# Taking the first four steps of a recurrence-and-network kernel apart into single operations, and reordering them

## The chip, the cores and the metric

The kernel runs on one core of one Trainium2 chip. The metric is device time in microseconds. The kernel before takes 613.97 us (median of three runs, 613.32 to 614.89). The engines are named as the profile names them: PE (matrix multiply, with PEld for its weight loads), DVE (vector), ACT (scalar), POOL (GpSimd) and SP (which here only issues transfers). Each works through its own queue of instructions in order, and waits where an instruction needs something that another engine or a transfer has not yet delivered.

## The reference

Two blocks are joined. The first is a gated linear recurrence over 768 time steps for 4 batches of 8 heads of width 48; the second is a network with one hidden layer of 2048 and a leaky activation, applied to its output:

```python
f = 1.0 / (1.0 + np.exp(-f_logit))
for t in range(S):                                  # S = 768
    state = f[:, :, t, :, None] * state + k_t outer v_t
    y[:, :, t] = q_t . state
x = y as (B*S, H*D)                                 # (3072, 384)
h = x @ w_in                                        # (3072, 2048)
g = np.maximum(h, 0.0) + alpha * np.minimum(h, 0.0)
out = g @ w_out                                     # (3072, 384)
```

The weights come in as 64-bit floats and are turned into 32-bit ones on the chip.

## The kernel before

The work is cut into twelve steps. A step is one pair of batches and one chunk of 128 time steps; steps 0 and 1 are the two pairs at the first chunk, steps 2 and 3 the same pairs at the second, and so on. A step has three parts. *Preparation* loads f, q, k and v, takes the sigmoid, builds products of the gates inside groups of four time steps ("lags"), scans over the groups, and forms the scaled q and k. *Attention* makes the scores on PE, copies them under masks, and multiplies with v. *Network* multiplies by `w_in`, applies the activation ("gates") and multiplies by `w_out`.

Each part is a table of small functions with short names. A single string of such names with step numbers gives the order: `FIRST` is written out for all pieces up to step 4's preparation and step 2's network, and `USUAL` is a pattern that repeats from step 4 on. The functions are called in that order, so the place of a name in the string is the place of its instructions in the queue of every engine that it uses. Nothing is reordered later. Semaphore waits are put in where data or a buffer is needed.

The names that matter here, with the lines of the kernel before. A letter `a` or `b` after a name is the half of step 0 (one batch each); a number after the colon is the step; a `V`, `A` or `G` at the end is the engine DVE, ACT or POOL.

- `ld` (L313 to L317) loads f, q, k and two halves of v, five transfers. Step 0 loads on SP's queue, steps 1 to 4 on POOL's. Each of these tiles has one buffer, so the load of f waits for the last reader of the previous step's f.
- `sg` (L320) sigmoid on ACT; `kr` (L321), `qc` (L322), `c0` to `c3` (L345) and `cg` (L347) copies on ACT; `l1`, `l2`, `l3` (recorded under L211, the helper for all elementwise products) the lags, two products each; `sc` (L353, L355) two scans on DVE; `le`, `k4`, `gk`, `nr`, `ke`, `sa`, `sb`, `e2` to `e7` further products at L211.
- `r` (L493), `h` (L553), `x` (L514), `kp` (L571), `of` (L597, L607), `pd`/`pz` (L635), `y` (L694), `t` (L717): the matrix products of attention on PE. `R` (L501) and `X` (L522, L538) are the masked copies of the scores on DVE, `H` (L559, L562) of some of them on ACT, `p` (L680), `oc` (L616, L618) and `s` (L429) the copies into the matrix `A` that `y` reads. `m` (L657 to L670) carries the state on. `z`, `T` and `mv` bring the result into the layout `xT` that the network reads.
- `id0` to `id7` and `jd0` to `jd7` (L235) load one eighth of `w_in` and of `w_out` each, 767 KB, into five buffers on SP's queue; `ih`, `il` (ACT, L240 and L243) and `ib`, `jb` (DVE, L211) turn it into 32-bit floats. A load waits until an earlier piece's `ih`/`il` has freed its buffer.
- The network of step 0 is `na`, `nb` (PE, L781), `ga`, `gb` (ACT, L787), `Ga`, `Gb` (DVE, L793, four instructions each), `va`, `vb` (L823), `o0`, `o1` (the result copies on ACT and their stores on SP). Later steps use `n0` to `n7` (L763), `g0` to `g7` (L769), `G0` to `G7` (L773, two instructions each), the sums `S0`, `S1` (four instructions each), and the products `A1`, `B`, `A2`, `C1`, `C2`, `D`, `E` (L859). `W` are differences of `w_out`, used from step 1 on.
- `kt` turns the keys of steps 2 and later on DVE; `km` moves them with sixteen small transfers on SP's queue, and `pd` waits for these.

So what decides the time of the opening is how five in-order queues, filled from one string, fit each other.

## Time and profile before

| | |
|---|---|
| median of the runs | 613.97 us (613.32 to 614.89) |
| span of the profiled execution, first to last instruction | 613.4 us |
| PE busy | 586.4 us, 96% of the span |
| DVE busy | 485.3 us, 79% |
| ACT busy | 242.5 us, 40% |
| POOL busy | 109.5 us, 18% |
| moved by DMA | 50.40 MB, mean 82 GB/s |
| first matrix product of the network (`na0:0`) starts | 39.32 us |
| step 4's first scores (`r0:4`), where the repeating pattern begins on PE, start | 191.19 us |

An engine's busy share over the whole span is an average over stages with different limits. The table of busy time by stretches is read first; then, for the stretch in which PE is not full, the timeline of each engine with the idle time before each instruction and what ended it.

### The profile page before, as it was taken

How to read it: one execution, taken by the hardware profiler on the slowest of the kernel's cores; microseconds unless marked ns; L12 is line 12 of the kernel's file. 1: busy time of each engine (PE TensorE's matmuls, PEld its weight loads, DVE VectorE, ACT ScalarE, POOL GpSimd, SP SyncE). 2: the span in 40 equal slices, each digit the busy share in tenths (PEclk: the TensorE clock that was granted, in tenths of full speed). 3: DMA queues.
4: the chain of work that ended last, by engine and by line, in shares of the span. 5: the costliest groups of instructions: out<-in, count | busy, mean ns of one | idle time of the engine just before them, and what ended most of it. 6: DMA issues, size and time to landing. Idle time of an engine off the chain costs nothing.

```text
span 613.4 us, 18759 instructions
## 1 busy us (share of the span) xinstructions
PE 586.4 (96%) x8042; PEld 526.6 (86%) x8042; DVE 485.3 (79%) x993; ACT 242.5 (40%) x464; POOL 109.5 (18%) x154
## 2 busy tenths in 40 slices
PE   1689899999999999999999999999999999999997
PEld 1589766898999799899899899889899889889997
DVE  7988899985588789799899799789799889762251
ACT  5887732523412352361272271361362263223110
POOL 7437566298050000000000000000000000000000
PEclk9999999999999999999999999999999999999999
DMA  8996343141002502502502502502602601201000
GB/s 272 322 337 186 103 142 53 41 136 24 14 25 45 153 10 43 158 2 49 161 1 50 159 2 47 162 2 42 168 1 39 162 11 35 47 2 27 26 1 26
DMA packets 72002, 50.40 MB, mean 82 GB/s; under 512 B 47248, under 2 KB 62480, under 8 KB 71920
## 3 DMA queue, kind: packets, MB, share of 16 engines
q1 hardware_dynamic: 64464, 38.77, 23.6%
q0 software_dynamic: 2944, 8.59, 4.8%
q10 hardware_dynamic: 4512, 1.85, 1.2%
q8 instruction: 63, 1.03, 0.8%
q14 instruction: 19, 0.16, 0.1%
HBM read 36.21 MB, written 4.72 MB: 67 GB/s over the span
## 4 chain that ended last, share of the span: by engine, by line
PE 84%; DVE 6%; ACT 3%; issue 2%; POOL 2%; DMA 2%; POOLq 0%; ACTq 0%; DVEq 0%
PE ph L763 32%; PE pc L859 10%; PE pa L859 9%; PE pe L859 5%; PE pd L859 5%; PE pb L859 5%; PE py L694 4%; PE phk L763 4%; PE qu L514 3%; PE raw L493 3%; DMA q<-in_qT 2%; PE ph L781 2%; PE state L635 2%; PE off L597 1%; DVE w_out_sb L211 1%
## 5 line engine op out<-in xcount | busy, mean ns | idle before, releaser
L763 PE MATMUL ph<-xT,w_in_sb 128*128 128x256 f32 x948 | 213.0, 382 | 0.0
L763 PEld LDWEIGHTS ph<-xT,w_in_sb 128*128 128x128 f32 x948 | 177.7, 190 | 27.0 <-issue 1.7
L769 ACT ACTIVATE neg<-ph 128x512 f32<-128x512 f32 x79 | 46.3, 597 | 146.7 <-PE ph L763 110.7
L773 DVE SCALAR_TENSOR_TENSOR gate<-neg,om,ph 128x256 f32<-128x256 f32 x158 | 67.7, 476 | 40.5 <-ACT neg L769 39.5
L731 POOL DMA_DIRECT2D xT<-y x22 | 11.9, 546 | 392.0 <-ACT y L703 392.0
L859 PE MATMUL pa<-w_out_sb,gate 128*128 128x192 f32 x352 | 61.9, 328 | 0.1
L859 PE MATMUL pc<-t,S 128*128 128x192 f32 x352 | 61.7, 329 | 0.0
L859 PEld LDWEIGHTS pa<-w_out_sb,gate 128*128 128x128 f32 x352 | 57.9, 190 | 2.0 <-DVE gate L773 1.3
L859 PEld LDWEIGHTS pc<-t,S 128*128 128x128 f32 x352 | 57.3, 190 | 0.8 <-issue 0.2
L522 DVE COPY_PREDICATED ad<-mquad,qu 128x224 f32<-128x224 int32 (+6 forms) x140 | 42.0, 300 | 9.3 <-PE qu L514 3.2
L501 DVE COPY_PREDICATED ad<-mraw,raw 128x256 f32<-128x256 int32 (+1 forms) x96 | 42.4, 441 | 7.0 <-POOL A L680 2.8
L345 ACT COPY ut<-qd 128x256 f32<-128x256 f32 (+1 forms) x52 | 32.0, 634 | 23.2 <-DVE qd L211 12.1
L211 DVE TENSOR_TENSOR ut<-ut,fs 128x512 f32<-128x512 f32 (+6 forms) x64 | 38.5, 604 | 3.3 <-POOL ut L211 2.4
L429 ACT COPY A<-q 48x512 f32<-48x512 f32 x40 | 24.7, 616 | 35.2 <-DVE q L211 31.9
L882 ACT ACTIVATE o<-pa 128x192 f32<-128x192 f32 x11 | 3.6, 330 | 76.9 <-PE pa L859 76.9
L493 PE MATMUL raw<-qd,k 48*32 48x80 f32 x1536 | 22.4, 243 | 10.3 <-DVE qd L211 10.3
L493 PEld LDWEIGHTS raw<-qd,k 48*32 48x32 f32 x1536 | 18.1, 109 | 15.7 <-issue 15.5
L680 ACT COPY A<-ad 32x256 f32<-32x256 f32 x75 | 30.1, 401 | 1.1
L859 PE MATMUL pe<-w_out_sb,S 128*128 128x192 f32 x176 | 30.5, 327 | 0.0
L859 PE MATMUL pb<-t,gate 128*128 128x192 f32 x176 | 30.4, 326 | 0.0
L859 PE MATMUL pd<-w_out_sb,S 128*128 128x192 f32 x176 | 30.4, 326 | 0.0
L694 PEld LDWEIGHTS py<-A,vs 128*64 128x64 f32 x768 | 26.0, 145 | 4.0 <-issue 2.2
(138 smaller groups left out, 894.3 us busy)
## 6 DMA issues: line engine op xcount, KB each, us to landing
w_out_raw<-in_w_out SPq DMA_DIRECT2D x8, 767.8 KB, 5.5
w_in_raw<-in_w_in SPq DMA_DIRECT2D x8, 767.2 KB, 12.1
out<-o SPq DMA_DIRECT2D x24, 192.0 KB, 2.1
f<-in_fT SPq DMA_DIRECT2D x7, 512.0 KB, 4.3
q<-in_qT SPq DMA_DIRECT2D x7, 512.0 KB, 5.2
k<-in_kT SPq DMA_DIRECT2D x7, 512.0 KB, 6.9
vs<-in_v SPq DMA_DIRECT2D x14, 192.0 KB, 6.9
ksn<-kt SPq DMA_DIRECT2D x80, 32.0 KB, 2.0
```

What stands on the lines that cost most here:

```text
L211: (nc.gpsimd if beside[0] else nc.vector).tensor_tensor(*a)
L345: w[f"c{r}{mark}"] = lambda r=r: nc.scalar.copy(q4()[:, gs, :, r], qdv[r][:, gs, :, 0])
L429: copy(A[halves(cc)[1], u0:u1, par * HP:(par + 1) * HP, CH * cc:CH * (cc + 1)], x["q3"][rows(par)].rearrange("p (u h c) s t -> p u h c (s ...
L493: nc.tensor.matmul(to[DB * j:DB * (j + 1), par, hp * C:hp * C + QW], lhsT=x["k"][r_, g * DB:(g + 1) * DB], rhs=qd[r_, g], start=True, stop ...
L501: nc.vector.copy_predicated(adu[:, :, :, d:4], mraw[:, d, :, d:4].bitcast(I32).unsqueeze(1).broadcast_to((128, H, NB, n_)), rv[:, :, QO[d] ...
L522: nc.vector.copy_predicated(ad[:, u, :, :, 4 * m:DB], mquad[:, lo:lo + n_].bitcast(I32).unsqueeze(1).unsqueeze(1).broadcast_to((128, 2, HP ...
L680: copy(A[s_, u, :, s_], ad[s_, u].rearrange("p r h t -> p (r h) t"))
L694: nc.tensor.matmul(to[64 * par:64 * par + 64, u, o:o + CH], lhsT=vs[bp][:, cc, u, hd * D:hd * D + 64], rhs=A[:, u, par * HP + hp, CH * cc: ...
L763: nc.tensor.matmul(ph[f][:, j * T:(j + 1) * T], lhsT=w_in_sb[:, kt, m * 128:(m + 1) * 128], rhs=x["T"][:, kt], start=(kt == 0 and j == 0), ...
L769: nc.scalar.activation(neg[f], ph[f].rearrange("p (j t) -> p j t", j=2), AF.Relu, scale=-1.0)
L773: nc.vector.scalar_tensor_tensor(gate[:, m % NH, m // NH], neg[f][:, j], om[:, m:m + 1], ph[f].rearrange("p (j t) -> p j t", j=2)[:, j], A ...
L859: nc.tensor.matmul(p[name][:, 0:DH], lhsT=of(f), rhs=by(f), start=(f == 0 and not more), stop=(f == NH - 1), skip_group_check=True)
```

## The change

`FIRST` becomes a new string. A helper `several` registers a list of operations under one name and each of them under a dotted name (`l1.0`, `l1.1`), and the pieces that held several instructions are taken apart with it: loads (5), lags (2 each), scans (2), the scaled keys `ke` (3), `sb` (2), `gk` (4), `nr` (3), the masked copies `R` (4), `X` (3 or 7) and `H` (3), the state copies `m` (2 or 3), the gates `G` (2 or 4) and the sums `S` (4). `USUAL` and all that follows from it stay as they were. Both programs hold the same 5978 instructions, with the same operands on the same engines; only their order in the queues differs.

```diff
 FIRST = """
-ldb:0 lda:0 id3V:0 id0V:0 id5V:0 id4V:0 id1V:0 sgb:0 qcb:0 l1bV:0 l2bV:0 l3bV:0 scb:0 c0b:0 sga:0 qca:0 l1aV:0 l2aV:0 l3aV:0 krb:0 sca:0 k4bV:0 fs:0
...
+ldb.0:0 C:0 sgb:0 l1b.0V:0 l2b.0V:0 ldb.1:0 qcb:0 c0b:0 krb:0 l1b.1V:0 lda.0:0 sga:0 lda.1:0 l3b.0V:0 l2b.1V:0 l3b.1V:0 cgb:0 ldb.2:0 l1a.0V:0 qca:0
+l1a.1V:0 gkb.0V:0 l2a.1V:0 c2b:0 l2a.0V:0 c1b:0 lda.2:0 l3a.1V:0 c3a:0 l3a.0V:0 id3V:0 lda.4:0 cga:0 kra:0 c3b:0 gkb.1V:0 scb.1:0 c2a:0 bl:0 gka.0V:0
+k4bV:0 k4aV:0 scb.0:0 c0a:0 c1a:0 sca.1:0 ih3:0 leaV:0 gka.1V:0 id4V:0 il3:0 lebV:0 gkb.2V:0 il4:0 keb.0V:0 id0V:0 il0:0 kea.1V:0 gka.3V:0 gka.2V:0
+r0:0 h0:0 H0.0:0 sca.0:0 H0.2:0 r1:0 gkb.3V:0 nra.0V:0 id5V:0 ldb.3:0 H0.1:0 h1:0 nrb.1V:0 nrb.0V:0 ih4:0 sabV:0 ldb.4:0 keb.2V:0 keb.1V:0 nra.1V:0
...
+    def several(w, name, ops):
+        w[name] = lambda: [op() for op in ops]
+        for n, op in enumerate(ops):
+            w[f"{name}.{n}"] = op
...
-            w["ld" + mark] = load
...
+            several(w, "ld" + mark, [lambda a=a: load(*a) for a in (("f", fT), ("q", qT), ("k", kT))]
+                    + [lambda cc=cc: load_v(cc) for cc in range(NC2)])
...
-            w["l1" + mark], w["l2" + mark], w["l3" + mark] = first_lag, second_lag, third_lag
+            several(w, "l1" + mark, [lambda: times(kr[:, qs, 1:2], f()[:, qs, 2:3], f()[:, qs, 3:4]), lambda: lagged(1)])
...
-            w["sc" + mark] = scans
+            several(w, "sc" + mark, [scan_on, scan_back])
...
+            several(w, f"R{u}", [lambda u=u, d=d: near_copies(u, d) for d in range(4)])
+            several(w, f"X{u}", [lambda u=u, m=m: quad_copies(u, m) for m in range(1, NB if c else NQ)])
...
+            several(w, f"G{f}", [lambda f=f, j=j: gates(f, j) for j in range(2)])
...
+            several(w, f"S{part}", [lambda part=part, m=m: sums(part, m) for m in range(4)])
```

In the queues this does the following. SP issues step 0's f and q of both halves first, then both k, and spreads the four v transfers between the loads of `w_in`; `w_out`'s `jd5` now goes before `w_in`'s `id2` and `id6`, and `jd2`, `jd4`, `jd0` before `id7`. POOL issues step 1's f and q as before, but k and v later, between other work. The store of `o0` stands before the sixteen transfers of `km:2` on SP, not behind them. DVE takes single gates, masked copies and products of different pieces in turn. PE does the same products in a partly different order.

237 lines of the change are left out of this document (116 added, 121 removed).

## Prediction

> **What bounds the kernel now.** I read the page's first two parts, then the table of busy time by stretches, the chain that ended last, and each engine's timeline over the first 72 us.
>
> ```profile
> PE 586.4 (96%) x8042; PEld 526.6 (86%) x8042; DVE 485.3 (79%) x993; ACT 242.5 (40%) x464; POOL 109.5 (18%) x154
> ```
>
> PE has 613.4 - 586.4 = 27 us to give at most. The stretches show where (columns: stretch, length, busy time of PE, PEld, DVE, ACT, POOL, clock, DMA share, GB/s):
>
> ```profile
> 0.00:20.00 20.00, 6.26 (x259) 5.44 (x260) 16.20 (x42) 11.32 (x24) 13.71 (x43) 1.00 0.92 300
> 20.00:40.00 20.00, 14.67 (x249) 13.05 (x248) 16.84 (x34) 17.47 (x38) 9.10 (x16) 1.00 1.02 320
> 40.00:60.00 20.00, 20.00 (x356) 19.48 (x362) 17.82 (x34) 16.55 (x31) 9.92 (x12) 1.00 0.73 233
> 60.00:80.00 20.00, 17.24 (x481) 14.72 (x482) 16.87 (x40) 16.41 (x30) 9.44 (x13) 1.00 0.26 81
> ```
>
> 19 us of the 27 are lost before 40 us, 2.8 between 60 and 80. From 80 on PE is busy 19.8 us of each 20 or more, but for 1.3 us lost near 207. The DMA share is 0.92 and 1.02 up to 40 us: the weights keep it full. So the time is when PE becomes full, plus what it loses later.
>
> In the chain, the opening hangs on one transfer, q of step 1, and later on two products on DVE:
>
> ```profile
> 15.63 11.38 DMA q<-in_qT
> ...
> 61.94 2.15 DVE kh L211
> 64.08 1.20 DVE ks L211 x2
> ```
>
> On ACT the copy of that q waits, and the copies that step 0's result needs stand behind it; PE waits for the last of them, and after 60 us for DVE and ACT:
>
> ```profile
> 27.03 1.04 ACT L322 COPY qd<-q 128x1024 f32<-128x1024 f32 x1 [0.64 <-DMA q<-in_qT]
> 28.10 1.65 ACT L680 COPY A<-ad 32x256 f32<-32x256 f32 x4
> ...
> 31.41 2.36 PE L694 MATMUL py<-A,vs 128*64 128x64 f32 x32 [0.70 <-ACT A L616]
> ...
> 65.44 0.63 PE L571 MATMUL keys<-ident,ks 128*128 128x128 f32 x4 [1.24 <-DVE ks L211]
> 66.47 0.63 PE L571 MATMUL keys<-ident,ks 128*128 128x128 f32 x4 [0.41 <-DVE gate L793]
> ...
> 68.41 0.29 PE L635 MATMUL keys<-vs,ksn 64*48 64x48 f32 x4 [0.47 <-ACT ksn L579]
> ```
>
> **The change, part by part.** No instruction is added or removed, so every price is a wait gained or lost. I walk the new queues with the durations of these timelines; successive instructions on one engine overlap by about 0.1 us there, and I count them so.
>
> *Up to `na0:0`, the point from which PE is full (39.32 us).* f of the second half is SP's third issue, not its sixth (about 1.7 us of issues, 0.43 to 0.6 each, come off); ACT had waited 2.50 us for it. DVE had slack there and gains about 1 us. ACT now puts `ih3`, `il3`, `il4`, `il0` (0.9 each) ahead of `H0`. The second weight load was ready at 15.6; `il0` needs the third, but about 0.4 MB of v no longer lies before it, so some 16.7. `H0` then ends at 18.4 (before: 18.41). DVE, with 18.7 us of rows ahead of `R0`, reaches it at 17.9 (rows overlap), so `R0` starts near 18.4, not at 21.48 as before; that is slack, since `R1`, `X` and `qc:1` come later. POOL issues step 1's f as soon as DVE's `le` is done, 13.3 against 14.72. If q needs its 11.4 us again it lands at 25.6, not 27.0. ACT's own work from `H0` to `qc:1` (`ih4`, `ih0`, `sg:1`, `H1`, `il5`, `ih5`, two `kc`) is 0.8+0.8+1.0+0.8+0.85+0.85+1.1 = 6.2 us, about 24.6 to 25.6 with the wait for f. `qc:1` ends at 26.7 (before 28.08). Four `oc` (0.7), four `p` (1.6) and `m0a` (0.6) follow without the `ih1` (0.9) and half the `oc` that stood among them, so `y0` starts at 29.8, not 31.41. After it ACT has four `oc`, `il1`, `ih1`, `c2:1`, `m0b`, `T01`, `T00`: 0.7+0.85+0.85+0.5+0.6+0.4 = 3.9, so 33.7; beside it PE does `y0`, waits for `z0V` and does `t0` until 33.3. `T02` on DVE now stands behind `gk.0:1`, which waits for `cg:1`, behind `ih2` on ACT: +0.9+0.2, then 0.5 on DVE. So `na0` starts at 35.3.
>
> The ends of this term: 35.3 if all goes so. If q lands at 27.0 all the same, +1.4. `jd5` is issued at about 14 in place of 20.2 for the next weight load and may push q and `id2` by its own 767 KB, at 320 GB/s 2.4 us; a later q and a late `id2` lie beside each other, so 35.3 to 39. I take 36.0, nearest to the walk: **3.3 us gained**.
>
> *From `na0:0` to `na3:0`.* The products between them are the same set (`t1`, `r:1`, six `na`/`nb`, `h`, `x`, `kp`, `r1:2`, `pd:1`, `of:1`), 30 us of PE. Before, PE waited 1.24+0.41+0.47 = 2.1 us here. After, DVE's rows from `T02` to `Gb1.0`, which `na3` needs, add up to 30.1 us with `kh` at its 2.2, 28.6 with it at 0.68: level with PE. So a wait of DVE passes to PE. I see two. `ga1` on ACT needs a free `neg` buffer, hence `Ga0.3`, and `Ga1.0` on DVE waits for it, 0.6 us. `ib7`, which `nb3` needs, is behind `il7` on ACT; both end near 53.8 with PE there at 53.5. I allow 1.2 us in all, between 0 and the 4 us that DVE's idle share of 40 to 80 us (5.3 of 40) would give over 30 us: **0.9 us gained**.
>
> POOL: nothing on PE waits early for k of step 1, now issued near 22 in place of 16.4; `r1:1` needs it at 40. POOL holds at f of step 2 until `kr:1` (45), before 47.08, so its products for step 2 run from 55 to 62.6 (before 52.94 to 63.53) and `r1:2` needs them at 63.6.
>
> *From `na3:0` to `r0:4`.* PE lost nothing here but 0.2 us. Its work, in either order, is equal. DVE stands at `X0.0:2` until `x0:2` is done; from there `pd:2`'s inputs are done 4.5 us early. `km:2` now waits on SP for `o0`'s store, which waits for `va3`; its sixteen issues took 11.54 us, and with 2.0 to land they end 1.5 us before `pd:2` needs them. `y1:2` needs `oc1:2`, 4.2 us of ACT's rows behind `g0:1`, where PE has 4.3 us between: level. POOL stands at f of step 3 until `le:2`, and the rest of step 2's products end near 80, 10 us early. At the end `C1:2` has 0.6 us over `S1.1V:2`, `x0:4` 2.4 us over `e7G:4`. I allow 0.2 us, between 0 and 2.
>
> *From `r0:4` (191.19) to the end*: same order, 422.2 us, same price.
>
> Sum: 613.4 - 3.3 - 0.9 + 0.2 = 609.4 us of span. The median of the runs is 0.6 above the profiled span, so **610.0 us**.
>
> [...] `kh` took 2.23 us while two POOL products ran, its like in later steps 0.68:
>
> ```profile
> 61.42 1.16 POOL L211 TENSOR_TENSOR fs<-f,kr 128x256 f32<-128x256 f32 x1
> 62.54 1.00 POOL L211 TENSOR_TENSOR qd<-qd,f 128x256 f32<-128x256 f32 x1
> ...
> 61.85 2.23 DVE L211 TENSOR_TENSOR kh<-k,ss 128x512 f32<-128x512 f32 x1
> 64.01 0.68 DVE L211 TENSOR_TENSOR ks<-k,ss 128x512 f32<-128x512 f32 x1
> ```
>
> [...]
>
> **The rivals.**
>
> *Slower: DVE and POOL block each other in the level stretch.* Place: DVE between 55 and 64 us, beside POOL's five products for step 2. Price: 2.23 - 0.68 = 1.55 us each, up to five, 7.8 us. For it: the row above, and DVE has no slack there. Against: DVE's masked copies beside POOL kept their 0.44, and only `sb.0:1` and `ke.1:1` there read two tiles. From three blocks on the gain is gone; from four it is slower; five give 613.97 - 4.0 - 1.2 (the allowance, replaced) + 7.8, about 616.5.
>
> *No change: `w_in`'s last eighth comes late.* `id7` is the twelfth weight load, not the sixth, and issued near 41, after `jl5`. ACT is at `ih7` at 47.2. The page gives the time from issue to landing:
>
> ```profile
> w_out_raw<-in_w_out SPq DMA_DIRECT2D x8, 767.8 KB, 5.5
> w_in_raw<-in_w_in SPq DMA_DIRECT2D x8, 767.2 KB, 12.1
> ```
>
> With 5.5 it is there at 46.7. With 12.1 ACT stands for 6 us, `nb3` starts about 4.3 later, and the time is 614.3. Against: 12.1 was measured while the queue was full, and 40 to 60 us has a share of 0.73.
>
> *More gained*: `na0` at 35.3 and no new wait: 613.4 - 4.0 - 2.1 + 0.6 = 607.9.
>
> That the change does not do what it says cannot be: the same instructions stand in another order.
>
> **How the numbers follow.** Forecast 0.45 (its own range 608.9 to 612.1), more gained 0.20, no change 0.16, slower 0.19. A measurement tells about 0.3%, 1.8 us, from no change. Forecast and more gained are faster by that: 0.65; same 0.16; slower 0.19. The range of 8 in 10 reaches from 606.5 (the walk with no allowance, and `r0:4` another 1.4 earlier) to 615.5, where most of the slower case begins.
>
> **What would show it.** `na0` starts at 35 to 37 us; `qc:1` does not wait beyond 26; PE's stalls between 60 and 72 us shrink below 1.5 us; `na3` starts near 67, `r0:4` near 187.2; from there 422 us to the end. I am wrong if ACT waits for q of step 1 or for a weight load beyond 27 us or at 47 us, if DVE's products at L211 run above 1.5 us between 50 and 64, or if PE waits at `pd:2`, `y1:2` or `C1:2`.

## The result, and the profile after

The changed kernel takes 622.56 us (median of 20 runs, 621.49 to 625.29), the kernel before 618.32 us in 20 runs on the same chip. The ratio is 1.0079, with a 95% interval of 1.0055 to 1.0103: slower by 0.8%, where 0.6% faster was predicted. The 613.97 us shown ahead is the median of the first three of these twenty runs before, which reach from 613.12 to 621.76 us; why they spread so far is not shown.

The profiled execution after has a span of 620.1 us, and its own time is 621.88. The profile of before has a span of 613.4 us; with the same 1.8 us on top it is of an execution of about 615.2, some 3 us quicker than the median. So the two traces differ by 6.7 us where the medians differ by 4.24. PE does the same work, in the page's first part:

```profile
PE 588.2 (95%) x8042; PEld 528.4 (85%) x8042; DVE 490.6 (79%) x993; ACT 242.2 (39%) x464; POOL 114.7 (18%) x154
```

By stretches (columns as in the table of before: length, busy time of PE, PEld, DVE, ACT and POOL, clock, DMA share, GB/s):

```profile
0.00:20.00 20.00, 6.62 (x200) 5.60 (x200) 18.48 (x48) 12.92 (x26) 14.23 (x42) 1.00 0.92 305
20.00:40.00 20.00, 9.17 (x259) 8.36 (x259) 9.00 (x21) 11.97 (x27) 6.43 (x12) 1.00 0.70 240
40.00:60.00 20.00, 19.97 (x353) 19.11 (x352) 17.73 (x33) 16.05 (x31) 7.46 (x12) 1.00 0.72 233
60.00:80.00 20.00, 16.79 (x378) 15.84 (x377) 19.32 (x40) 13.89 (x27) 14.00 (x16) 0.83 0.41 147
```

Between 20 and 40 us PE is busy for 9.17 us; before it was 14.67. Between 60 and 80 it is busy for about as long as before, but at a clock of 0.83. The starts of the pieces on PE that the prediction used say where the time went (worked out from the two traces):

```
piece    before   predicted   after    stretch from the row above: before / predicted / after
y0:0      31.41      29.8      35.57
na0:0     39.32      36.0      43.63    7.91 /   -    /  8.06
na3:0     71.31      67        78.11   31.99 / 31.1   / 34.48
r0:4     191.19     187.2     198.56  119.88 / 120.1  / 120.45
end      613.4      609.4     620.1   422.2  / 422.2  / 421.5
```

From `na3` on the prediction holds. Nearly all of the loss lies ahead of `na0` (4.31 us) and between `na0` and `na3` (2.49 us). The chain that ended last has both, and a piece called "issue", a time in which the engine waited for nothing that the profile shows:

```profile
13.50 9.33 DMA f<-in_fT
...
27.73 1.44 PE off L614 x21
29.16 3.29 issue
...
63.88 5.50 DVE ks L223
```

On ACT, `sg:1` now waits for f of step 1, and the copy of q, `qc:1`, comes when everything behind `sg:1` is done:

```profile
22.91 1.06 ACT L339 ACTIVATE f<-f 128x1024 f32<-128x1024 f32 x1 [4.14 <-DMA f<-in_fT]
...
27.56 1.06 ACT L341 COPY qd<-q 128x1024 f32<-128x1024 f32 x1
```

On PE, the timeline has the hole inside `of:0` at 32.45, then the wait at `x1:1` and three pieces that take longer than their like in the run with `ke.1` early below (1.40, 1.15 and 1.09 us):

```profile
32.45 0.79 PE L614 MATMUL off<-q,kh 48*64 48x64 f32 x10 [3.29 <-issue]
...
35.57 0.48 PE L703 MATMUL py<-A,vs 128*64 128x64 f32 x4
...
43.63 2.94 PE L790 MATMUL ph<-xT,w_in_sb 128*128 128x128 f32 x24
...
70.39 1.84 PE L524 MATMUL qu<-ut,k 48*32 48x52 f32 x128 [3.11 <-DVE gate L801]
72.32 1.97 PE L614 MATMUL off<-q,kh 48*64 48x64 f32 x32
74.23 1.97 PE L578 MATMUL keys<-ident,ks 128*128 128x128 f32 x8
```

The wait at `x1:1` ended with a gate on DVE (L801, done at 70.36), which came right behind the last masked copy, `R1.3:1`. Both stood behind a single product on DVE, `ke.1:1`; its like takes 0.68 us elsewhere:

```profile
63.80 5.58 DVE L223 TENSOR_TENSOR ks<-k,ss 128x512 f32<-128x512 f32 x1
```

POOL beside it (the first row is the issue of a load, the others are products of step 2):

```profile
62.98 0.75 POOL L330 DMA_DIRECT2D k<-in_kT  x1
63.75 0.74 POOL L223 TENSOR_TENSOR ut<-ut,fs 128x256 f32<-128x256 f32 x1
64.44 1.94 POOL L223 TENSOR_TENSOR qd<-qd,f 128x768 f32<-128x768 f32 x1
66.35 1.14 POOL L223 TENSOR_TENSOR kr<-f,kr 128x256 f32<-128x256 f32 x1
67.45 2.75 POOL L223 TENSOR_TENSOR qd<-qd,f 128x512 f32<-128x512 f32 x2
```

So there are four things to explain: the hole at 29.16, the late f, the product of 5.58 us, and the clock. `na0` to `na3` has one more oddity: PE's clock record falls to 0.5 at 70.05 and returns at 76.87.

### The profile page after: what moved, and what is told of

It is laid out like the page before. It is cut to its first block, busy times and chain, and to the rows that moved or that the text cites. A ratio compares the mean times of both kernels' runs of the same rounds, so it can differ in the third digit from the quotient of the medians.

```text
span 620.1 us, 18763 instructions
## 1 busy us (share of the span) xinstructions
PE 588.2 (95%) x8042; PEld 528.4 (85%) x8042; DVE 490.6 (79%) x993; ACT 242.2 (39%) x464; POOL 114.7 (18%) x154
## 3 DMA queue, kind: packets, MB, share of 16 engines
q8 instruction: 63, 1.03, 0.7%
## 4 chain that ended last, share of the span: by engine, by line
PE 86%; DVE 7%; issue 2%; DMA 2%; POOL 1%; ACT 1%; POOLq 0%; ACTq 0%
PE ph L772 32%; PE pc L867 9%; PE pa L867 9%; PE pe L867 5%; PE pd L867 5%; PE pb L867 5%; PE py L703 4%; PE phk L772 4%; PE qu L524 3%; PE po L832 3%; PE raw L504 3%; DMA f<-in_fT 2%; PE state L642 1%; PE off L604 1%; DVE ks L223 1%
## 5 line engine op out<-in xcount | busy, mean ns | idle before, releaser
L531 DVE COPY_PREDICATED ad<-mquad,qu 128x64 f32<-128x64 int32 (+6 forms) x140 | 41.6, 299 | 9.8 <-PE qu L524 4.4
L511 DVE COPY_PREDICATED ad<-mraw,raw 128x256 f32<-128x256 int32 (+3 forms) x96 | 41.9, 441 | 7.1 <-ACT ad L569 4.5
L223 DVE TENSOR_TENSOR ut<-ut,fs 128x512 f32<-128x512 f32 (+6 forms) x64 | 35.2, 554 | 3.4 <-ACT ut L357 1.6
L524 PE MATMUL qu<-ut,k 48*32 48x112 f32 (+1 forms) x1536 | 25.3, 265 | 8.7 <-DVE ut L223 5.6
L504 PE MATMUL raw<-qd,k 48*32 48x80 f32 x1536 | 22.8, 246 | 8.7 <-DVE qd L223 8.7
L504 PEld LDWEIGHTS raw<-qd,k 48*32 48x32 f32 x1536 | 18.4, 110 | 14.7 <-issue 14.4
L871 DVE SCALAR_TENSOR_TENSOR Csum<-pc,Csum 128x192 f32<-128x192 f32 x22 | 7.9, 357 | 28.6 <-PE pc L867 28.4
```

Of the source, the lines that this page charges most:

```text
L223: (nc.gpsimd if beside[0] else nc.vector).tensor_tensor(*a)
L504: nc.tensor.matmul(to[DB * j:DB * (j + 1), par, hp * C:hp * C + QW], lhsT=x["k"][r_, g * DB:(g + 1) * DB], rhs=qd[r_, g], start=True, stop ...
L511: nc.vector.copy_predicated(adu[:, :, :, d:4], mraw[:, d, :, d:4].bitcast(I32).unsqueeze(1).broadcast_to((128, H, NB, n_)), rv[:, :, QO[d] ...
L524: nc.tensor.matmul(to[DB * j:DB * (j + 1), par, o + 4:o + width], lhsT=x["k4"][r_, g * DB:(g + 1) * DB], rhs=x["us"]()[r_, g, 4:width], st ...
L531: nc.vector.copy_predicated(ad[:, u, :, :, 4 * m:DB], mquad[:, lo:lo + n_].bitcast(I32).unsqueeze(1).unsqueeze(1).broadcast_to((128, 2, HP ...
```

## The experiments

### The hole: PE waits for its own program

The trace holds 63 transfers named "instruction" on a queue of their own, 1.03 MB in all, 16,384 bytes each. PE has 16,313 instructions in the trace, about 256 for each transfer. Counting PE's instructions in blocks of 256 and laying the transfers beside them gives this table (us; worked out from the traces, so which transfer belongs to which block is inferred from the times):

```
kernel   a block is entered   next block's transfer   last of the old block   PE goes on
before        12.05              15.63 - 16.58              18.76              18.76
before        18.76              22.48 - 23.58              27.21              27.22
after         15.44              19.34 - 20.47              25.82              25.83
after         25.83              29.92 - 31.00              28.85              32.45
```

In these rows, with the weights filling the queues, a block's transfer begins 3.6 to 4.1 us after the block ahead of it was entered and takes 0.95 to 1.13 us; where PE stood, it goes on 1.3 to 1.7 us after its end. For blocks entered between 38 and 50 us the transfer begins 0.5 to 1.6 us after that; for later ones it begins anywhere from 3.7 us before to 5.4 us after, so the moment of asking is only inferred. Before, PE spent its blocks of the first 40 us slowly, with 2.2 us or more to spare; the new order puts `x1:0`, `of:0` and `pd:0` together, PE passes 256 instructions in 3 us, and the transfer that by the count brings the next ones ends 2.15 us after that.

The count agrees in every trace of the whole computation. PE stands for "issue" by more than 0.3 us at 29 places in the fourteen traces, and each is at instruction 193 + 256n, with n a whole number and matmuls and weight loads counted together (worked out from the traces); the hole here is at 705. Two of them are in the kernel before, 0.45 us at 69.95 and the 1.3 us near 207 that the prediction names; after, that one is 0.50 us:

```profile
208.54 0.30 PE L635 MATMUL state<-vs,ksn 64*48 64x48 f32 x6 [1.27 <-issue]
```

```profile
215.22 0.30 PE L642 MATMUL state<-vs,ksn 64*48 64x48 f32 x6 [0.50 <-issue]
```

To test it I gave PE more instructions and nothing else to do: two more copies of `h1:0`, whose results are written again with the same values.

```diff
- ... ldb.3:0 H0.1:0 h1:0 nrb.1V:0 ...
+ ... ldb.3:0 H0.1:0 h1:0 h1:0 h1:0 nrb.1V:0 ...
```

> The changed kernel with step 0's product h1:0 done three times over, one after the other, while PE has nothing else to do (18 to 25.6 us): 32 products that write the same values again, nothing moved. Theory A (PE's own program arrives too late: 256 instructions, or 64 of these products, were used up between 25.83 and 28.85 us, and the 16 KB that follow were asked for at 25.83 and had landed at 31.00): with 32 products more ahead of it, that point of the program is passed at about 19.5 us, so the next 16 KB are there by 25, and the 3.6 us hole inside of:0 (28.85 to 32.45) is gone. A later hole of up to 1.5 us may appear in pz or pd near 32. y0:0 starts at 31.9 to 33, not at 35.57, and the kernel is 2 to 3.6 us faster than the changed one: ratio to the kernel before about 1.002 to 1.005 where the changed one has 1.0079. Theory B (the hole is a wait for data, such as v or the scaled keys, or for a transfer that lands near 32 us): the added products change nothing there, the hole still ends at 32.4, y0:0 at 35.6, ratio 1.008.

Ratio 1.0156 (1.0127 to 1.0185). The holes moved with the count of instructions and became three ahead of `y0`, with no wait on data (a fourth, of 1.67 us, stands at 51.67):

```profile
22.44 1.17 PE L561 MATMUL raw<-ut 48*64 48x32 f32 x34 [3.18 <-issue]
...
29.34 0.84 PE L524 MATMUL qu<-ut,k 48*32 48x52 f32 x43 [1.58 <-issue]
...
35.17 0.72 PE L642 MATMUL state<-vs,ksn 64*48 64x48 f32 x11 [1.20 <-issue]
```

The first stands in the middle of the added products: block entered at 15.83, transfer 19.79 to 20.91, last old instruction 18.97, PE goes on at 22.44. So the hole follows the count of PE's instructions, and PE goes on 1.53 us after the transfer's end. The gain that I expected of the edit did not come: PE stood at two later boundaries as well.

Two edits test what stood ahead of the hole. In the first, DVE does `nrb.2:0` and `nra.2:0`, for which `x1:0` waited until 25.64, ahead of `R1.0:0`. In the second, ACT does `sg:1` right before `qc:1`, so that nothing stands behind its wait for f.

```diff
- ... il5:0 R1.0:0 ... id2V:0 nrb.2V:0 nra.2V:0 id6V:0 ...
+ ... il5:0 nrb.2V:0 nra.2V:0 R1.0:0 ... id2V:0 id6V:0 ...
```

> The changed kernel with two products of DVE (nrb.2 and nra.2 of step 0, 0.29 us each) moved ahead of the masked copy R1.0:0, which waits for ACT until 24.86; DVE stood idle from 20.36 to there. x1:0 on PE needs them. Theory A (PE's program arrives too late): x1 starts at 20.9 instead of 25.64, the program's boundary inside x1 is passed near 21.1, the next 16 KB land near 26.3 and of:0, which still waits for ksn on ACT until 27.7, has no hole. y0:0 starts near 31.7, na0:0 near 40 instead of 43.63; 3 to 4 us faster than the changed kernel, ratio about 1.002. Theory B (the hole waits for data or a transfer that comes at 32.4): the hole stays, y0:0 at 35.6, ratio 1.008.

```diff
- ... kpa:0 sg:1 R0.1:0 ... x1:0 qc:1 ...
+ ... kpa:0 R0.1:0 ... x1:0 sg:1 qc:1 ...
```

> The changed kernel with the sigmoid sg:1 on ACT moved from before H1:0 to just before qc:1. In the changed kernel ACT stood 4.14 us at sg:1 for step 1's f, which landed at 22.83, with H1, il5, ih5 and kc (5.7 us) behind it. Now H1 ends at 19.6, kc at 22.5, sg:1 runs at 22.9 and qc:1 ends between 25.0 and 26.6 instead of 28.62. Theory A (PE's program arrives too late): DVE reaches nr.2 near 21, x1 starts at 21.3, the boundary is passed at 21.4 and the next 16 KB are there only at 26.6; PE uses up its 64 products at about 24.4, so the hole does not go, it lies at 24.4 to 28 instead of 28.85 to 32.45: y0:0 at about 31.2 instead of 35.57, na0:0 near 39.2, 4.4 us faster than the changed kernel, ratio about 1.001. If the hole were none of the program's (theory B, data that come at 32.4): y0:0 stays at 35.6 and the ratio at 1.008. If only ACT's wait had cost anything (theory C), y0:0 at 28 and ratio 0.996.

Ratios 1.0053 (1.0033 to 1.0073) and 1.0056 (1.0038 to 1.0074). The groups of runs stood on different chips, with medians of before from 615.58 to 619.1 us, and the changed kernel was not run again with them, so the ratios of two groups compare only to about 0.5%. Single traces differ as well: `na0` came between 43.63 and 44.63 in four kernels whose order up to there is the same, so a difference under 1 us between two traces means little. Each edit brought `y0` forward, to 32.94 and 33.41 from 35.57, and neither as far as 29.8. In the first the hole inside `of:0` went, and one of 0.68 us stood inside `x1:0`, at an earlier boundary; `of:0` waited for ACT until 28.55, that is, for f:

```profile
22.29 1.63 PE L524 MATMUL qu<-ut,k 48*32 48x52 f32 x106 [0.68 <-issue]
...
28.55 2.05 PE L614 MATMUL off<-q,kh 48*64 48x64 f32 x31 [4.64 <-ACT ksn L586]
```

In the second ACT was in time, PE reached its block's end at 25.42, and the hole grew:

```profile
30.27 0.80 PE L614 MATMUL off<-q,kh 48*64 48x64 f32 x10 [4.54 <-issue]
```

So the late f and the hole are two limits side by side: taking one away shows the other.

### The late f

POOL issued f of step 1 at 13.50, 1.22 us earlier than before. From issue to landing (last column, us), before:

```profile
f<-in_fT POOLq DMA_DIRECT2D x1, 512.0 KB, 7.8
q<-in_qT POOLq DMA_DIRECT2D x1, 512.0 KB, 11.4
```

and after:

```profile
f<-in_fT POOLq DMA_DIRECT2D x1, 512.0 KB, 9.3
q<-in_qT POOLq DMA_DIRECT2D x1, 512.0 KB, 12.8
```

14.72 + 7.8 = 22.5 before, 13.50 + 9.3 = 22.8 after: the earlier issue bought nothing. The first packet of POOL's queue moved at 18.89 before and at 18.47 after; until then the queue of the weights had the engines, at a share of 1.04 before (12 to 18.8 us) and 1.06 after (12 to 18.4 us). I took it for the added `w_out` load and put three loads behind `qc:1`, on ACT's queue.

```diff
- ... H1.1:0 jd5V:0 ... kcb:0 id2V:0 ... id6V:0 ... qc:1 ...
+ ... H1.1:0 ...     ... kcb:0 ...               ... qc:1 id2A:0 jd5A:0 id6A:0 ...
```

> The changed kernel with three weight loads (jd5, id2, id6; 767 KB each, issued on SP's queue at 12.8, 18.0 and 18.8 us, their readers at 42 to 47 us) issued later, on ACT's queue behind qc:1. Nothing else is moved. Theory F (step 1's f and PE's own program come late because these loads fill the DMA engines): f of step 1, issued at 13.5, lands near 19 to 20 and not at 22.83; the lag from the passing of a 256-instruction boundary to the start of its 16 KB transfer falls from 3.9 to 4.1 us towards the 0.8 to 1.5 us of the quiet stretches after 40 us; x1:0 starts near 21.6, the hole inside of:0 shrinks from 3.6 us to 1.5 or less, y0:0 near 29.7 instead of 35.57, na0:0 near 38; about 5 us less than the changed kernel, ratio to the kernel before about 0.999 where the changed one has 1.0079. Theory G (f and the program take their time whatever else is on the queues): f at 22.8, lag near 4 us, y0:0 near 35.6, ratio 1.008 to 1.010 (ACT pays three issues).

f landed at 22.97 all the same, its first packet at 19.01; ratio 1.0032 (0.9999 to 1.0065). The theory that these three loads push f falls. What holds POOL's queue until 18.5 may have been issued earlier still, the first loads of `w_in` and step 0's own; that is argued from the bytes per queue, not shown, and a full share of the engines alone doesn't explain it: after, step 2's f was issued at 53.99 beside a share of 0.95 and moved its first packet 1.46 us later. The loads do push q: q of step 1 landed at 24.43 in place of 27.21. The other part of the edit that helped was another: with fewer bytes queued, the transfer of the program's block began 2.2 us after the block ahead of it was entered instead of 4.1, and the hole was 1.10 us.

### The product of 5.58 us

`ke.1:1` and `sb.0:1` moved ahead, behind `ke.2:1`, so that DVE is done with them before POOL's products of step 2 begin.

```diff
- ... ke.2V:1 sg:2 ... R1.1:1 sb.0V:1 R1.2:1 Gb0.3:0 ke.1V:1 jd6V:0 ...
+ ... ke.2V:1 ke.1V:1 sb.0V:1 sg:2 ... R1.1:1 R1.2:1 Gb0.3:0 jd6V:0 ...
```

> The changed kernel with two of DVE's products of step 1 moved: ke.1:1 (5.58 us in the changed kernel, 63.80 to 69.38, with four products of POOL back to back beside it; its like takes 0.69) and sb.0:1 go to just behind ke.2:1, near 62 us, before POOL begins its run at 63.75. Theory D (a DVE product that reads two SBUF tiles gets no turn while POOL's products follow each other without a gap): ke.1 takes 0.7 to 1.4 us, R1.3:1 ends near 66 instead of 70.24, x1:1 on PE starts at 67.3 with no wait instead of 70.39, and the time is about 3 us less: ratio 1.0079 - 0.005 = 1.003. The rival (E: ke.1 is slow for a reason of its own, such as the transfers of w_out near 64 us, or PE stood for something else): ke.1 is slow in the new place too, or x1:1 still starts near 70, ratio 1.008.

Ratio 1.0056 (1.0036 to 1.0076). The product took its usual time, PE didn't wait at `x1:1`, and the clock stayed at 1.0:

```profile
62.47 0.70 DVE L223 TENSOR_TENSOR ks<-k,ss 128x512 f32<-128x512 f32 x1
```

```profile
67.74 1.40 PE L524 MATMUL qu<-ut,k 48*32 48x52 f32 x128
69.21 1.15 PE L614 MATMUL off<-q,kh 48*64 48x64 f32 x32
70.29 1.09 PE L578 MATMUL keys<-ident,ks 128*128 128x128 f32 x8
```

From `na0` to `r0:4` it took 151.74 us, against 154.93 in the changed kernel and 151.87 before. The place is settled, and its price is 3.2 us: 4.46 us gained up to `na3`, of which 1.27 were given back up to `r0:4`.

What kept DVE out for so long is another question. A kernel that leaves the computation out and measures the meeting by itself missed it: DVE's product began ahead of POOL's run, at 14.39 against 15.15, and took its usual 0.69 us.

> Nothing of the computation is left but a measurement; the output is zeros. One DVE product (128x512, two SBUF operands) starts some 0.6 us after POOL begins a run of 0, 1, 2, 4 or 6 products of the same size, each with no wait between them; then, beside four products, a DVE product with one operand in PSUM, and a DVE copy; all three times over. Theory D (no turn while POOL's run lasts): 0.7 us alone, and beside N products it ends when the run ends, so about 1, 2, 4.5 and 7 us for N = 1, 2, 4, 6; the one with a PSUM operand and the copy keep their 0.4 to 0.7 us. [...]

In the next one DVE's product comes due inside POOL's run of one, two, four or six products, all contiguous.

> As e8, which missed: there DVE's product began before POOL's run, and POOL waited for it. Now DVE's product is released four ACT copies after POOL's run, so it arrives inside the run. Nothing of the computation is left, the output is zeros. Groups, three times over: runs of 1, 2, 4, 6 POOL products (1.3 us each); four with a one-column memset between them; four beside a DVE product with one operand in PSUM; four beside a DVE copy. Theory D (DVE gets no turn until POOL's run is over): DVE's product takes, from its release, about 0.7, 1 to 2, 4 to 5 and 7 us with the four runs; with the memsets between it gets in at the first gap, so 1.5 to 2 us; 0.7 and 0.43 us for the product with a PSUM operand and the copy. [...]

Beside four products (17.60) and six (25.05), on DVE:

```profile
17.60 1.45 DVE L69 TENSOR_TENSOR dout<-then,x 128x512 f32<-128x512 f32 x1 [4.66 <-ACT then L67]
25.05 1.45 DVE L69 TENSOR_TENSOR dout<-then,x 128x512 f32<-128x512 f32 x1 [6.00 <-ACT then L67]
```

In that kernel POOL's products wrote the same tile and stood 0.08 us apart, so the theory could still hold for a run without gaps: DVE gets in only where POOL leaves one, and its product lasts to the end of the run. With different tiles, so that POOL's next product starts as the last one ends:

> e9 with one difference: POOL's products of a run write different tiles, so that none waits for the one before. Output zeros, nothing of the computation is left. [...] The rival (turns by instruction, and ke.1's 5.58 us came from its own access pattern): 1.45 us at most, as in e9.

DVE took 1.32, 1.33 and 1.32 us beside two, four and six, whose runs lasted 2.48, 5.38 and 7.82 us. So it did not wait for the end of the run, with gaps in it or without: both theories fall. Next, the form of the operands: POOL's lags read rows out of longer rows, and `ke.1` multiplies by one value for every four.

> Nothing of the kernel is computed here and the output is zeros: POOL does runs of five products, and DVE's product comes due some us into the run. POOL's forms: contiguous (128x512), or the lags' (rows of 2 out of rows of 4, and the real sequence of 256, 768, 256, 512, 256 elements). DVE's forms: contiguous, or that of `ke.1` (blocks of 32 out of 64, by one value for every four). Alone, DVE's product took 0.63 to 0.69 us. Theory D3 (the form of the operands decides; with POOL's strided products or DVE's broadcast operand DVE doesn't get in at the first boundary): one of the pairings that has a lag or the form of `ke.1` shows 3 us or more for DVE's product, as the 5.58 us in the changed kernel, and the contiguous pairing 1.3 to 1.5. [...] If neither form brings 3 us, what kept `ke.1` for four products stays open.

Beside the lags' sequence, one product of `ke.1`'s form took 1.93 us, and three of them in a row 4.73, 1.6 each:

```profile
70.31 1.93 DVE L85 TENSOR_TENSOR d<-k,ss 128x512 f32<-128x512 f32 x1 [10.08 <-ACT k L98]
...
89.95 4.73 DVE L85 TENSOR_TENSOR d<-k,ss 128x512 f32<-128x512 f32 x3 [5.96 <-ACT k L98]
```

No pairing came near 5.58. Left was the load that POOL issues just ahead of its products. In the kernel itself, that issue moved behind them:

```diff
- ... jh2:0 ld.2:2 Gb0.2:0 ... l3.1G:2 l3.0G:2 r1:2 ...
+ ... jh2:0 Gb0.2:0 ... l3.1G:2 l3.0G:2 ld.2:2 r1:2 ...
```

> The changed kernel, with POOL's issue of step 2's k (`ld.2:2`, at 62.98 us, just ahead of the products beside which `ke.1:1` took 5.58 us) moved behind those products. Theory D4 (the load's issue on POOL is what keeps DVE out): `ke.1:1` takes 0.7 to 2.3 us, `x1:1` doesn't wait, and PE is at `na3` 3 us or so earlier, unless `r1:2`, which reads that k, then waits for it. If the products alone do it: 5.5 us again, and PE waits 3 us at `x1:1`.

On DVE:

```profile
64.60 0.75 DVE L223 TENSOR_TENSOR ks<-k,ss 128x512 f32<-128x512 f32 x1
```

and on PE:

```profile
68.10 1.40 PE L524 MATMUL qu<-ut,k 48*32 48x52 f32 x128
...
76.16 1.33 PE L504 MATMUL raw<-qd,k 48*32 48x80 f32 x64 [4.55 <-DMA k<-in_kT]
```

`ke.1:1` took 0.75 us and `x1:1` didn't wait. PE then waited 4.55 us for the k that the moved load brings, so nothing was won (one run, 624.17 us). This agrees with the load as the cause, but doesn't prove it: in this run DVE came to its product 0.78 us after POOL's first product had started, in the changed kernel 0.05 us after. The last kernel was to part the two by themselves:

> Nothing of the kernel is computed and the output is zeros: POOL does one small product, then (in every second half of the groups) issues a load, then the series of the changed kernel at that place: a product by a broadcast value (256 elements), 768, 256, 512 and 256 elements in the lags' form. DVE does copies out of PSUM and comes to its one product of 128x512 at different times around the start of the series, contiguous or in the form of `ke.1`. If the meeting at the series' start, or the load's issue ahead of it, is what costs: one of the groups shows 4 us or more for DVE's product, D4 in the groups with the load alone. If not: 0.7 to 2.7 us in all groups, and the cause stays open.

It did not: the loads were issued away from the products they should have stood ahead of, and DVE's contiguous product always met the series 0.2 us after the small product; it took 1.09 us. So the cause of the 5.58 us stays open between the load and the moment of meeting, which no run parts. The block came in seven kernels, the run with more `h0:1` and the one with another opening below among them, and took 5.58 to 5.68 us. Each time the load stood right ahead of POOL's products, DVE's product began within 0.05 us of the first of them, and it ended 0.56 us after POOL's fourth, where POOL left its first gap (68.82 to 68.90 in the changed kernel). In the run with the old opening below, the load did not stand right ahead and DVE came 1.41 us after POOL's first product had begun: it took 1.96 us, though POOL left no gap there.

### The clock

My theory was that the hole of 3.1 us at `x1:1` lets the clock fall. Ahead of `x1:1` I put three more `h0:1`, whose results are written again, so that PE is busy for most of the hole.

```diff
- ... H0.2:1 R0.0:1 ...
+ ... H0.2:1 h0:1 h0:1 h0:1 R0.0:1 ...
```

> The changed kernel with step 1's product h0:1 done three times more between nb1:0 and x1:1 on PE, where PE stood still for 3.11 us (67.28 to 70.39) because DVE's R1.3 was late: 48 products that write the same values again, some 1.7 us, no data come earlier. In the changed kernel's trace TensorE's clock falls to 0.5 at 70.05 and is back at 76.87; x:1, of:1 and kp:1 take 1.84, 1.97 and 1.97 us there, against 1.40, 1.15 and 1.09 in e4, whose clock stayed at 1.0. Theory H (the hole's length brings the half clock, and the half clock costs as much again): the hole is now about 1.4 us, the clock stays at 1.0, x1:1 starts near 70.4 as before, and from there to na3:0 it takes 6 us instead of 7.7: 2 us faster than the changed kernel with more work done, ratio about 1.0045. The rival (I: the clock falls for another reason at that place, or the slow products are slow because of POOL and DVE beside them): clock and times as in the changed kernel, ratio 1.008.

Ratio 1.0112 (1.0082 to 1.0142): the hole shrank to 1.28 us, and the clock fell all the same, at 71.36, for 6.83 us.

```profile
67.66 1.60 PE L565 MATMUL raw<-ut 48*64 48x32 f32 x96
70.54 1.60 PE L528 MATMUL qu<-ut,k 48*32 48x52 f32 x128 [1.28 <-DVE gate L805]
```

As put, the theory fails. So the clock by itself, in a kernel that computes nothing: runs of 66 products of 128x128x128, some 16 us each, and between them waits or small products.

> Nothing of the computation is left; the output is zeros. PE does 66 products of 128x128x128 (about 16 us at full clock), then stands for some 1, 2.5, 4.5 and 6 us in turn, or does 96 or 192 products of 48x64x32 (3 and 6 us) instead; all four times over. Theory H2 (the clock is judged by the work done in windows of 3.41 us: in the changed kernel 27.31 us at full clock are 8 of these, 6.83 us at half clock are 2): 1 us never brings the half clock, 6 us always, 2.5 to 4.5 us by how the hole lies to the windows, and full clock lasts whole multiples of 3.41 us. If small products count as little as standing still, 192 of them bring the half clock too, and 96 sometimes; if any product counts, neither does.

The small products stood free in the queue and were taken into the waits, so the run has no empty hole: it measures stretches of 2.4 to 23.4 us of products of 48x64x32, between runs of large ones:

```profile
22.27 5.41 PE L72 MATMUL small<-y 48*64 48x32 f32 x80
27.61 17.63 PE L60 MATMUL big<-y,x 128*128 128x128 f32 x132
```

All stretches of the clock record but the last of a run, which the record's end cuts short, are multiples of 3.41 us: in the changed kernel 27.31, 6.83 and 542.72, in the kernel before 573.44. Laying the large products on a grid of 3.41 us (worked out from the trace; columns: the window of 3.41 us; the share of it with large products; the work of all its products, large and small, where each matmul row of the trace counts as rows times columns of its weights times columns that stream, in units of one of 128x128x128; the clock from its end on):

```
 22.91 -  26.32   0.00    2.7   falls to 0.5
 26.32 -  29.73   0.62    9.3   stays at 0.5
 29.73 -  33.15   1.00   16.1   back to 1.0
156.03 - 159.44   0.37   11.6   stays at 1.0
173.09 - 176.51   0.34   10.04  falls to 0.5
302.80 - 306.21   0.36   11.2   stays at 1.0
319.86 - 323.28   0.34    9.9   falls to 0.5
```

In the first window PE is busy with small products all the time, and the clock falls. The share of large products does not decide it by itself: in other kernels windows with a share of 0.05 to 0.18 stayed at 1.0, and 0.58 brought the clock back in the run with `sg` later, where 0.62 did not here. The work fits. Of the 2514 windows of the fifteen traces with a clock record, from the first recorded rise on, the 70 after which the clock is 0.5 hold 10.04 at most, and the 2444 after which it is 1.0 hold 10.25 at least, whether the clock was up or down (worked out from the traces). This is a fit and not a mechanism: ahead of the first rise, two windows of 10.5 and 11.5 did not bring it.

The fit holds for both runs. In the changed kernel the window from 66.63 to 70.05 has PE idle from 67.28 on and holds 5.0, and the clock falls at its end; that from 73.46 to 76.87 holds 11.5, and at its end the clock is back at 1.0. In the run with more `h0:1` the window from 67.95 to 71.36 holds 6.9, since a product of 48x64x32 counts 0.047. So by this fit the hole does let the clock fall, because too little work is left in the window, and what I put into the hole was too little work. The price is read from the three rows at 70.39 to 74.23 against those of the run with `ke.1` early: 1.84 + 1.97 + 1.97 against 1.40 + 1.15 + 1.09, 2.1 us. Up to `na3` only 1.1 us of it count, because at full clock PE waits there instead, 0.65 and 0.34 us.

### Which half of the order

The order of before up to `na0:0`, and the changed order for the rest (no diff is shown: the string up to `na0:0` is that of before, with the names of several operations written out one by one):

> The order of the kernel before up to and with na0:0, and from there the changed order of what is left: one part of the change alone. If the two losses are independent, the times of the two profiles add: na0:0 at 39.3 as before, from there to na3:0 34.5 us as changed (before 32.0), to r0:4 120.4 (before 119.9), to the end 421.5: a span of 615.7 against 613.4, ratio about 1.004, with a DVE product of step 1 blocked beside POOL's run and PE waiting some 3 us at x1:1. If the later loss came only from the opening's lateness (a shifted meeting of DVE and POOL), the block is gone and na3:0 is reached 30 us after na0:0: ratio 0.996.

and the same with `ke.1` and `sb.0` early:

> As e6, with ke.1:1 and sb.0:1 of step 1 moved to just behind ke.2:1 on DVE as in e4. If the sum holds: na0:0 39.3, to na3:0 30.0 (as e4's profile has it), to r0:4 121 to 121.7, to the end 421.7: a span of 612 to 612.7, ratio 0.998 to 0.999. If the kernel before is only hard to beat because its opening suits its own later part (weights of step 0 converted at other places), na0 to na3 is again 32 us or more and the ratio 1.002 or above.

Both 1.0025 (0.9990 to 1.0061). `na0` came at 41.13 and 38.04, though the two have the same order up to there, so single traces of this opening differ by 3 us. `na0` to `na3` took 36.2 and 34.1 us, where the second should have shown 30. With the old opening q of step 2 is issued late, and ACT stands before it, with `ga1` and `ib7` behind (the row is of the second):

```profile
55.32 1.05 ACT L345 COPY qd<-q 128x1024 f32<-128x1024 f32 x1 [5.71 <-DMA q<-in_qT]
```

So the halves can't be priced by exchanging them; the second is made for the first.

### Together, and a new opening

The three moves above (`nr` early, `sg` later, `ke.1` and `sb.0` early) and `r1:0` ahead of `h0:0`:

> The changed kernel with the moves of e2, e3 and e4 together, and r1:0 ahead of h0:0 on PE, so that PE's program passes its first boundary at about 10.5 us instead of 15.4. If the causes are the ones named (program, ACT behind f, DVE beside POOL's run with the half clock behind it): no hole at x1:0, which starts near 21; the next 16 KB of the program are asked for near 21.2 and usable near 28 to 29, so of:0 ends near 30; y0:0 at 31.5 to 32.5, na0:0 near 40 to 41, x1:1 without a wait, na3:0 30 us after na0:0, r0:4 near 192, clock 1.0 to the end: a span of 613 to 614, ratio 0.999 to 1.002. If the moves do not add (each only uncovers the next wait), ratio 1.004 or more.

Ratio 0.9955 (0.9929 to 0.9981), 615.24 us: `y0` at 31.64, `na0` at 40.41, `na3` at 70.56. The hole is still there, 3.15 us: its block is entered at 22.08, the transfer runs from 25.97 to 27.06, and PE has spent the block at 25.05.

```profile
28.51 0.80 PE L618 MATMUL off<-q,kh 48*64 48x64 f32 x10 [3.15 <-issue]
```

What is left is to let PE enter its blocks earlier. In the last version the products that need nothing new stand as early as their data allow (`r1`, `x1`, `x0`, and `kp` of both halves together), so that the block is entered at 16.99 instead of 22.08; `sg:1` and `qc:1` stand behind the copies that step 0's result needs. `ke.1` and `sb.0` stand early. Two lines are added, which keep the order of a buffer.

```diff
- r0:0 h0:0 H0.0:0 sca.0:0 H0.2:0 r1:0 ... kea.2V:0 kpa:0 sg:1 R0.1:0 ... kcb:0 id2V:0 nrb.2V:0 nra.2V:0 id6V:0 ld.2:1 x1:0 qc:1 ...
+ r0:0 r1:0 h0:0 ... nra.1V:0 nrb.2V:0 nra.2V:0 ... x1:0 x0:0 ld.0:1 ... kpa:0 kpb:0 R0.1:0 ... kcb:0 id2V:0 id6V:0 ld.2:1 s10b:0 s11b:0 sg:1 ofb:0 ...
...
+            if not n:
+                got("pk", psf)
```

> The changed kernel with its opening (from r0:0 to na0:0) put in another order by what the runs have shown, and e4's two moves: r1 before h0, nr.2 at once, x1 and x0 ahead of kp (so that the program's boundary inside x1 is passed near 18 us and the next 16 KB are usable near 24.6), sg:1 behind kc on ACT, qc:1 and the lags that need it behind all that y0 needs, POOL's copies for y1 ahead of l3:1. The buffer of kp's result is taken before that of x's, so that of:0 waits for kc as before. If the causes are the ones named: x1:0 near 17 to 18, of:0 done near 26, y0:0 near 29, na0:0 near 36 to 37, na3:0 30 us later, r0:4 near 188, span 609 to 611, ratio 0.993 to 0.997. If the opening is bound by the transfers instead (q of step 1, the program), na0:0 stays near 40 and the ratio near 1.0.

Ratio 0.9919 (0.9887 to 0.9950), 611.94 us: faster than both kernels. There is no hole ahead of `na0` (transfer 21.05 to 22.18, block spent at 24.64; two of 0.34 and 1.26 us stand later, at 66.28 and 442.5), and no wait at `x1:1`:

```profile
28.50 0.48 PE L709 MATMUL py<-A,vs 128*64 128x64 f32 x4
...
35.93 2.94 PE L796 MATMUL ph<-xT,w_in_sb 128*128 128x128 f32 x24
...
60.54 1.40 PE L530 MATMUL qu<-ut,k 48*32 48x52 f32 x128
```

And the new opening alone, with `ke.1` where the change has it:

> e12's opening with ke.1:1 and sb.0:1 back where the change put them. From the profiles: na0:0 near 36 as in e12 (35.93), then DVE's ke.1 beside POOL's run again, PE waiting near x1:1, the half clock behind it, na3:0 some 34 us after na0:0 in place of 31.2, so a span of 613 to 615 and a ratio of 0.995 to 0.998, 0.003 to 0.006 above e12's 0.9919. If the block was only a matter of when DVE and POOL happen to meet, which the new opening shifts: ke.1 at 0.7 us and the ratio of e12.

Ratio 0.9946 (0.9923 to 0.9969), 614.95 us. `ke.1:1` took 5.62 us again, `x1:1` waited 3.15 us, and the clock fell to 0.5 at 65.06. `na0` to `r0:4` took 155.31 us against 152.87 with it early: 2.4 us for the product and the clock, in a kernel without a hole ahead of `na0`.

## Why the prediction was wrong

**The walk up to `na0:0` (3.3 us gained, measured 4.31 lost).** It gave 35.3, and 43.63 was measured: 8.3 us off, in three steps.

- *"PE does `y0`, waits for `z0V` and does `t0` until 33.3"*, and `na0` at 35.3: 5.5 us from `y0` to `na0`. The profile of before has 7.91 for the same stretch (31.41 to 39.32), and after it was 8.06. The rows of before give 2.36 for `y0`, 0.88 of waiting and 2.90 for `t0`, 6.1 us where the walk has 3.5, and the walk left out `y1` (1.92), which PE does ahead of `na0` in both orders. So 2.6 of the 8.3 us are a wrong addition, nearly all of it refuted by the rows of before. With before's 7.91 the walk gives 37.7 and a gain of 1.6 us.
- *"If q needs its 11.4 us again it lands at 25.6."* It needed 12.8 and landed at 27.2, and f needed 9.3 in place of 7.8: issued 1.22 us earlier into a full queue, f landed at 22.8 against 22.5. The walk named this end (q at 27.0, +1.4 us) and didn't take it. ACT stood 4.14 us at `sg:1`, `qc:1` ended at 28.62 and not at 26.7, and without the hole `y0` would have been at about 32.3 (35.57 less the hole), 2.5 us later than walked. The end for `jd5`, which "may push q", was right as well: with the loads put later q landed at 24.43. The sign that I gave, `qc:1` waiting beyond 26, didn't show by its letter: `qc:1` waited for nothing, because the wait had moved ahead of it, to `sg:1`.
- *The hole*, 3.3 us: no term, no rival and no bound had it. The page's third part lists PE's instruction transfers, for before too, and I had read them as no cost, since up to 40 us they had 2.2 us or more to spare. Before's own profile had the sign, the 1.3 us near 207 that the prediction names and the 0.45 at 69.95, both "issue". A change that only reorders was said to have no price but waits on data; here it also had the 3.29 us of "issue" that came after PE had passed 256 instructions in 3 us.

**`na0` to `na3` (0.9 us gained, measured 2.49 lost).** The waits of before did go, and `ga1`'s and `ib7`'s did not come: with `ke.1` early the stretch takes 30.02 us, even less than the 31.1 predicted. The rival "DVE and POOL block each other" took the gain. Its place, the stretch beside POOL's products of step 2, and one of its two candidates, `ke.1:1`, were right; `sb.0:1` stayed at 0.40. Its price was thought of as up to five blocks of 1.55 us; it was one block of 5.58 - 0.68 = 4.9 us, three of the blocks by which "the gain is gone". The products measured by themselves beside a series of POOL's took 0.69 to 1.97 us; what makes this one so much longer no run shows. The fall of the clock, another 1.1 us up to `na3`, was in no term.

**`na3` to `r0:4` (0.2 us lost, between 0 and 2)**: 0.57 measured, within its ends. PE had no wait worth naming at `pd:2`, `y1:2` or `C1:2`, as the sums of DVE's, POOL's and SP's rows had said. **From `r0:4` on** 422.2 us were predicted and 421.5 measured.

**The rival of the late `id7`** did not come: `ih7` stood at 55.35 without a wait.

The forecast of 610.0 lies 12.6 us below the median, and the range ended at 615.5. About 4 us of this are in the comparison itself, 618.32 for before and not 613.97. The 0.6 us added for the median compared two different executions; each recorded run stands 1.7 to 2.0 us above its own span. On the profiled spans, 609.4 was forecast and 620.1 measured: 8.3 - 0.7 ahead of `na0` (35.3 had been moved to 36.0), 3.4 between `na0` and `na3`, 0.4 after it, and 0.7 back at the end. That the walk's goal was within reach is shown by the new opening: `na0` at 35.93, the time at 611.94 us.

## What to carry to other kernels

Before an order is judged by its waits on data, count how fast the new order lets PE spend its instructions: here it packed small products together while the queues were full, PE passed 256 instructions in 3 us and then stood for 3.29 us, and the only sign was "issue" ahead of a row with no releaser. Such rows stood in the profile of before (0.45 and 1.27 us), and were worth a look however short. An earlier issue into a full queue is worth nothing until a row shows that it lands earlier (here f, issued 1.22 us earlier, landed 0.3 us later); and a walk should first be laid on the profile of before, stretch by stretch, since a sum that doesn't give the known time won't give the new one. A DVE product that must not be late shouldn't stand beside a series of POOL's: here one of 0.68 us took 5.58 us there.

## What the hardware showed that I had not expected

- PE can stand with all its data there. The 63 transfers named "instruction" are of 16,384 bytes each, one for about 256 of PE's 16,313 instructions. In the opening the next transfer begins 3.2 to 5.1 us after a block of 256 is entered, for most blocks entered before 32 us; holes of 0.3 to 4.5 us followed where PE spent a block sooner, all at instruction 193 + 256n. Where PE's order was slow enough, as in the kernel before up to 40 us, with 2.2 us or more to spare, no hole came. That entering a block is what asks for the next is inferred from the times.
- The stretches of the clock record are multiples of 3.41 us (27.31, 6.83, 542.72, 573.44), and it stood at 0.5 while PE was busy: through stretches of up to 23.4 us of products of 48x64x32. What fits all windows after the first rise is the work in one, with the point between 10.04 and 10.25 matmuls' worth of 128x128x128, for falling and for returning; this is a fit to these traces. Ahead of the first rise PE is slower, too: in the changed kernel the clock record begins with a rise at 42.74, and twelve rows of `xt` take 2.90 us at 39.52 and 1.50 us at 46.41, though the table of stretches prints 1.00 for the opening.
- One DVE product of 0.68 us stood for 5.58 to 5.68 us beside a series of POOL's products, in seven kernels; contiguous and strided products measured by themselves took 0.69 to 1.97 us beside such a series. Moving the load that POOL issued ahead of the series took it away (0.75 us), but moved the meeting as well, so the cause is open.
